# Chunked linear attention feeding a top-1 expert layer: loads of a chunk at other times and from two queues, a state update moved, a count folded into another product

## The chip, the core and the metric

The kernel runs on one core of one Trainium2 chip. The metric is device time in microseconds, from start to end of one execution; the figure used is the median of a few executions.

## What is computed

Two stages follow each other. The first is a linear attention with a decaying state, for 4 batches, 8 heads, 768 tokens and head size 48:

```python
for t in range(S):
    kt, vt, rt = (k[:, :, t], v[:, :, t], r[:, :, t])
    cur = np.einsum('bhd,bhe->bhde', u[None] * kt, vt)
    y[:, :, t] = np.einsum('bhd,bhde->bhe', rt, state + cur)
    state = w[None, :, :, None] * state + np.einsum('bhd,bhe->bhde', kt, vt)
```

Its output, 3072 tokens of 384 numbers, goes through a layer of 8 experts. Each token is sent to the expert with the largest logit, and there `out[mask] = gate_w[mask, None] * eom[mask, e, None] * (np.maximum(x[mask] @ w1[e], 0) @ w2[e])`, with the softmax weight of the chosen expert and a sigmoid gate.

## The kernel before, in words

The attention works on 24 chunks of 128 tokens, six along the sequence for each of four batches, with the batch running fastest. A chunk i is cut into two halves of 64 tokens, so that a decaying state is carried twice per chunk. The loop over chunks starts at line 1432, and its body is an order written out by hand: in the schedule in force each engine runs its instructions in just the order in which the code names them, and semaphores make it wait where data are not ready. Iteration i finishes the output of chunk i and prepares the chunks that follow. In it stand, in this order:

- `product(i+2)` on GpSimd (POOL, line 274), `scale(i+3)` on VectorE (DVE, line 261), `carry(i+1, 1)`, the second state update of chunk i+1 (a DVE addition that reads PSUM at line 336, then a POOL multiplication at line 337), and `keys(i+3)` on POOL (line 267).
- `strips(i+1)` (line 1378): small matmuls on TensorE (PE) for the bonus coefficients (line 373) and the router's logits (line 461), and two copies on ScalarE (ACT, lines 1388 and 469).
- `logits_t`, three transposes on PE (line 451) and an ACT copy (line 453), then `bonus(i+1)`, eight ACT instructions at line 382.
- `intra(i)` on PE (line 363) and `output(i)`: the DVE addition `x` at line 389, and the store of `x` to the scratch `x_d` from the SP queue (line 390).
- `state(i+2)` (PE, line 317) and `scores(i+1)` (PE, line 291), which fill one pair of PSUM banks; `carry(i+2, 0)` (lines 336 and 337); `inter(i+1)` (PE, line 353), which writes into the one pair of banks that the addition `x` of chunk i reads; and `causal(i+1)` (DVE, line 297), which masks the scores.

The pair of banks of `state` and `scores` has one buffer. So `state(i+2)` may start only when `causal(i)`, `carry(i+1, 0)` and `carry(i+1, 1)` have read the pair before. Likewise `inter(i+1)` may start only when `x` of chunk i has been read out.

Each chunk needs four loads, all issued from the SP queue by `load` (line 1272): the two halves of `rk` (192 KB each), `k` and `v` (200 KB each). They go into rings of 5, 4 and 5 buffers. In iteration i SP issues, behind the store of `x`: the second half of `rk` of chunk i+5, `v` of chunk i+5, `k` of chunk i+6 and, behind `causal`, the first half of `rk` of chunk i+6. No load is left from iteration 19 on.

The router's work is woven into the loop. Its tokens are taken in five groups of 5, 5, 4, 4 and 6 chunks (`GROUPS`). The program of a group (`Router.group`, line 477) is a generator that yields what its next step needs: a slot on DVE, a place for PE (`P`) or ACT (`A`), or a wait for PE's result (`W_`). `micro(i)` (line 1367) adds a credit from `BUDGETS` and runs DVE steps, 0.15 of credit each, until it is used up; `exchange` and `resume` run the others at fixed points of the iteration. A group's steps are: argmax and one-hot, the gate, the ranks' product on PE (lines 572 to 576), ranks and one-hot of positions with the weighting between them (`side`), the table's product on PE (line 631), and its additions to the table. For the group that ends at chunk 14 the generator `order` (line 713) runs before the gate: a PE product that sums the counts of each expert, a wait, and six DVE steps that find the fullest expert, whose number SP reads to load that expert's weights early (`load_raw`). From iteration 18 on, `weights0` splits these weights on ACT and POOL. After the loop come the experts, eight slots of matmuls.

Of the kernel before, what the change touches and what calls it, by code (L numbers as in the profile page):

```python
# [2 lines left out]

# [10 lines left out]
ALU = mybir.AluOpType  # L14
# [14 lines left out]
E, F = 8, 1024  # L29
# [20 lines left out]
ORDER_AT = 14  # L50
# [3 lines left out]
V, P, A, W_, SPLIT = "vector", "tensor", "scalar", "wait", "split"  # L54
SPLITS = {18: 1, 19: 1, 20: 1, 21: 1, 22: 2, 23: 2}
RINGS = {"rk": 5, "k": 4, "v": 5}
PARTS = {"rk": (0, RKW), "k": (RKW, RKW + NAT), "v": (RKW + NAT, IN)}
BUDGETS = [[0, 0.3], [12, 0.45], [18, 0.9], [20, 1.3]]
TAIL = 3
# [334 lines left out]
class Router:  # L394
# [82 lines left out]
    def group(self, ps, w, lg, i0, G, closing, last):  # L477
        nc, k = self.tc.nc, self.k
# [37 lines left out]
        cs = self.csum  # L516
        if not last:
# [5 lines left out]
            else:  # L523
                nc.vector.tensor_add(self.csum, self.csum, cs)
        if i0 + G == ORDER_AT and not self.plain:
            yield from self.order(ps, w)

# [47 lines left out]
        for c in range(G - 1):  # L575
            nc.tensor.matmul(cnt[:, (c + 1) * E :], k.ones16, oh16[:, c, :].unsqueeze(1).to_broadcast((C, G - 1 - c, E)), start=False, stop=(c == G - 2), skip_group_check=True)
        yield W_
        rk = mk("rk", E)
        cv = cnt.rearrange("p (c e) -> p c e", e=E)
# [132 lines left out]

    def order(self, ps, w):
        nc, k = self.tc.nc, self.k
        yield P
        pt = self.room[:, self.pt :]
        nc.tensor.matmul(pt[:, :E], k.ones, self.csum, start=True, stop=True)
        yield W_
        key = self.okey
        nc.vector.scalar_tensor_tensor(key, pt[:, :E], float(E), k.desc, op0=ALU.mult, op1=ALU.add)  # L720
        yield V
        top = w.tile([C, 1], F32, name="top")
        nc.vector.tensor_reduce(out=top, in_=key, axis=AX.X, op=ALU.max)
        yield V
        nc.vector.tensor_scalar(self.pm0, key, top, None, op0=ALU.is_ge)
        nc.vector.tensor_scalar(self.opm, key, top, None, op0=ALU.is_ge)
        yield V
        pe = w.tile([1, E], F32, name="pe0")
        nc.vector.tensor_mul(pe, self.opm[0:1], k.ip[0:1, :E])
        yield V  # L730
        pr = self.opr[0:1]
        nc.vector.tensor_reduce(out=pr, in_=pe, axis=AX.X, op=ALU.add)
        yield V
        nc.vector.tensor_copy(self.eid[:, 0:1], pr)
        self.after_order()
        yield V
# [513 lines left out]
def rwkv_top1_moe(ctx, tc, rkv, wu, wg, w1, w2, r, kk, v, w, u, out):  # L1250
    nc = tc.nc
# [10 lines left out]
    with ExitStack() as actx:  # L1262
# [8 lines left out]

        def load(nm, i, j=None):
            if i < NT:
                a, z = PARTS[nm]
                rows = slice(0, C) if j is None else slice(HB * j, HB * j + D)
                nc.sync.dma_start(rings[nm][i % RINGS[nm]][rows], rkv[i, rows, a:z])

# [81 lines left out]
        def mark():  # L1359
            gates[0] += 1  # L1360
            return gates[0]

        def resume():
            if pend and pend[0][1] == W_:
                pend[0][1] = V
# [8 lines left out]
        def exchange(kind):  # L1374
            if pend and pend[0][1] == kind and passed[0] > asked[0]:
                step()

        def strips(i, cs):
            lg = ps.tile([C, 512], F32, name="ps_cf", tag="lg", bufs=1)
            if i < NT:  # L1380
                att.coefs(i, lg)
            prog = None
            if i >= LATE:
                dst, prog = slot(i - LATE)
                pl = lg[:, 32 * E : SPARE]
                rt.logits_into(pl, xTs.pop(i - LATE))
            if i < NT:
                nc.scalar.copy(cs, lg[:, :E])  # L1388
            if i >= LATE:
                rt.logits_out(pl[:, : 2 * E], dst)  # L1390
            if prog:
                pend.append([prog, V])
            return lg
# [29 lines left out]
        att.state(1)  # L1423
        load("k", 1 + RINGS["k"])
        att.carry(1, 0)
        att.keys(2, nc.gpsimd)
        att.scale(2)
        x = None
        xTs = {}

        masked = mark()
        for i in range(NT):
            tail = i == NT - 1
            att.product(i + 2)
            att.scale(i + 3)
            att.carry(i + 1, 1)
            att.keys(i + 3, nc.gpsimd)
            micro(i)
            lg = strips(i + 1, cs[(i + 1) % 2])
            exchange(A)  # L1440
            if x is not None:
                xTs[i - 1] = rt.logits_t(ps, rw, x, "lg" if tail else "l", 1)
            exchange(P)
            att.bonus(i + 1, cs[(i + 1) % 2])
# [10 lines left out]
            exchange(P)  # L1455
            load("rk", i + RINGS["rk"], 1)
            load("v", i + RINGS["v"])
# [3 lines left out]
            att.state(i + 2)  # L1461
            load("k", i + 2 + RINGS["k"])
            att.scores(i + 1, range(NP - 1))
# [7 lines left out]
            passed[0] = summed  # L1471
            att.causal(i + 1)
            resume()
            load("rk", i + 1 + RINGS["rk"], 0)
            load_raw(1)
            micro(i, 2)
            if tail:
                ex.early_mm(ps, 0)
            for _ in range(SPLITS.get(i, 0)):
                weights0(pieces.pop(0))  # L1480
                micro(i)
            masked = mark()
        dst, prog = slot(NT - 2)
# [108 lines left out]
```

## Time and profile before

| | us |
|---|---|
| median of 3 runs | 401.1 (400.38 to 403.56) |
| profiled execution, its own time | 406.86 |
| its span, first to last instruction | 405.1 |

| engine | busy us | share of the span |
|---|---|---|
| PE | 358.9 | 89% |
| PE weight loads | 336.8 | 83% |
| DVE | 224.5 | 55% |
| ACT | 169.8 | 42% |
| POOL | 155.1 | 38% |

The table is an average over two stages with different limits: the chunks up to about 160 us, and the experts behind them. The profiled execution took 5.8 us longer than the median of the runs shown.

### The profile page before, as it was taken

Reading aid. Unit: us, or ns where it says so; the run is one execution under the profiler, and the core shown is the slowest. Engines: PE = TensorE matmul, PEld = TensorE weight load, DVE = VectorE, ACT = ScalarE, POOL = GpSimd, SP = SyncE. Lnnn points to the kernel's source line nnn. Section 1 sums busy time; section 2 is a strip of 40 time slices with the busy share of each in tenths; the row PEclk is TensorE's granted clock in tenths of the full one; section 3 lists DMA queues with packets and bytes.
Section 4 is the critical chain, followed back from the end, with each engine's and each line's share of the span. In section 5 each row is a group of like instructions: output and inputs, shape, how many; then the busy total and the mean of one; then the engine's idle time right before and its main releaser. Section 6 shows DMA issues by size and latency. Waiting matters only on the chain. (4 is left out here: it accounts for less than half of the span.)

```text
span 405.1 us, 12806 instructions
## 1 busy us (share of the span) xinstructions
PE 358.9 (89%) x5186; PEld 336.8 (83%) x5186; DVE 224.5 (55%) x565; ACT 169.8 (42%) x479; POOL 155.1 (38%) x214
## 2 busy tenths in 40 slices
PE   7796888786988867997999999999999999999990
PEld 3695777776877766887899999999999999999990
DVE  6553569668778762845763374374373653726600
ACT  3443444342444435522443263363553533634400
POOL 7754464643665617624150412312322412413010
PEclk9888998997998989999999999999999999999996
DMA  7946654763578206063372463454463563634110
GB/s 278 312 138 183 197 165 130 212 180 106 164 209 253 97 23 183 14 214 91 90 228 80 127 187 119 135 181 122 137 213 120 160 230 116 229 113 117 64 44 19
DMA packets 26516, 60.58 MB, mean 150 GB/s; under 512 B 4143, under 2 KB 13411, under 8 KB 26448
## 3 DMA queue, kind: packets, MB, share of 16 engines
q1 hardware_dynamic: 23024, 49.85, 40.6%
q0 software_dynamic: 3424, 9.82, 7.2%
q8 instruction: 43, 0.70, 0.7%
q14 instruction: 25, 0.20, 0.2%
HBM read 50.22 MB, written 9.76 MB: 148 GB/s over the span
## 5 line engine op out<-in xcount | busy, mean ns | idle before, releaser
L943 POOL DMA_INDIRECT out_dram<-yo,si x28 | 31.0, 1106 | 133.9 <-ACT yo L940 69.8
L906 PE MATMUL ps_h<-xh,w1h 128*128 128x384 f32 (+4 forms) x216 | 72.2, 334 | 0.8 <-DVE yo L942 0.8
L907 PE MATMUL ps_h<-xl,w1h 128*128 128x384 f32 (+4 forms) x216 | 70.7, 328 | 0.0
L908 PE MATMUL ps_h<-xh,w1l 128*128 128x384 f32 (+4 forms) x216 | 70.7, 327 | 0.0
L855 DVE TENSOR_TENSOR w1l<-raw,w1h 128x768 fp32r<-128x768 f32 x28 | 26.1, 955 | 61.0 <-ACT w1h L854 61.0
L915 ACT ACTIVATE hh<-ps_h 128x384 fp32r<-128x384 f32 (+4 forms) x72 | 34.1, 475 | 46.2 <-PE ps_h L908 45.4
L916 DVE SCALAR_TENSOR_TENSOR hl<-ps_h,hh 128x384 fp32r<-128x384 f32 (+4 forms) x72 | 38.4, 534 | 24.8 <-ACT hh L915 22.9
L382 ACT ACTIVATE vc<-v,cs 128x48 f32<-128x48 f32 x192 | 45.9, 324 | 0.1
L877 POOL DMA_INDIRECT xg<-x_d,gi x28 | 30.8, 1099 | 38.4 <-PE ps_xt L889 26.0
L337 POOL TENSOR_TENSOR T<-Ts,sq 128x192 f32<-128x192 f32 x40 | 20.2, 506 | 64.7 <-DVE Ts L336 59.7
L968 PE MATMUL ps_o<-w2h,hh 128*128 128x384 f32 x128 | 43.8, 342 | 0.7 <-ACT yo L940 0.7
L970 PE MATMUL ps_o<-w2h,hl 128*128 128x384 f32 x128 | 42.8, 335 | 0.0
L969 PE MATMUL ps_o<-w2l,hh 128*128 128x384 f32 x128 | 42.8, 334 | 0.0
L906 PEld LDWEIGHTS ps_h<-xh,w1h 128*128 128x128 f32 x216 | 40.7, 189 | 1.5 <-issue 1.1
L907 PEld LDWEIGHTS ps_h<-xl,w1h 128*128 128x128 f32 x216 | 40.8, 189 | 0.1
L908 PEld LDWEIGHTS ps_h<-xh,w1l 128*128 128x128 f32 x216 | 40.7, 188 | 0.1
L1388 ACT COPY cs<-ps_cf 128x8 f32<-128x8 f32 x24 | 4.0, 165 | 75.4 <-PE ps_cf L461 67.2
L363 PEld LDWEIGHTS ps_y<-v,A 64*64 64x64 f32 x768 | 27.3, 147 | 7.1 <-issue 3.0
L363 PE MATMUL ps_y<-v,A 64*64 64x64 f32 x768 | 31.1, 234 | 2.3 <-DVE A L297 1.4
L274 POOL TENSOR_TENSOR rk<-rk 128x512 f32<-128x512 f32 x24 | 30.5, 1272 | 0.7 <-DMA rk<-in_rkv_dram 0.7
L261 DVE TENSOR_TENSOR rk<-rk,ps_tb 128x1024 f32<-128x1024 f32 x24 | 28.9, 1211 | 0.7 <-ACT ps_tb L228 0.7
L291 PE MATMUL ps_a<-rk 48*64 48x64 f32 x768 | 25.8, 239 | 3.3 <-issue 2.9
(206 smaller groups left out, 722.8 us busy)
## 6 DMA issues: line engine op xcount, KB each, us to landing
raw<-in_w_dram SPq DMA_DIRECT2D x64, 384.0 KB, 3.5
rk<-in_rkv_dram SPq DMA_DIRECT2D x38, 192.0 KB, 4.0
k<-in_rkv_dram SPq DMA_DIRECT2D x24, 200.0 KB, 4.5
v<-in_rkv_dram SPq DMA_DIRECT2D x24, 200.0 KB, 3.6
x_d<-x SPq DMA_DIRECT2D x24, 192.0 KB, 1.9
rk<-in_rkv_dram SPq DMA_DIRECT2D x5, 512.0 KB, 5.6
xg<-x_d,gi POOLq DMA_INDIRECT x28
out_dram<-yo,si POOLq DMA_INDIRECT x28
```

The source lines that it names most:

```text
L363: nc.tensor.matmul(o, A[rows, j, q, :], self.values(i, rows, 2 * q + j), start=(i < B and c == 0 and q == 0), stop=(q == NP - 1), skip_gro ...
L382: nc.scalar.activation(vc[:, h, :], vt[:, h, :], AF.Copy, scale=cs[:, h : h + 1])
L877: nc.gpsimd.indirect_dma_start(out=self.xg[q][:n], out_offset=None, in_=self.x_d[:n_x, :], in_offset=bass.IndirectOffsetOnAxis(ap=self.rt. ...
L906: nc.tensor.matmul(o, wh[:, j, fs], xh, start=(j == 0), stop=False)
L907: nc.tensor.matmul(o, wh[:, j, fs], xl, start=False, stop=False)
L908: nc.tensor.matmul(o, wl[:, j, fs], xh, start=False, stop=(j == KC - 1))
L915: nc.scalar.activation(hh, o, AF.Relu)
L916: nc.vector.scalar_tensor_tensor(hl, o, 0.0, hh, op0=ALU.max, op1=ALU.subtract)
L943: nc.gpsimd.indirect_dma_start(out=self.out, out_offset=bass.IndirectOffsetOnAxis(ap=self.rt.si[:n, q, s : s + 1] if s else self.rt.si0[:n ...
L968: nc.tensor.matmul(o, hh, wh, start=(f == 0), stop=False)
L969: nc.tensor.matmul(o, hh, wl, start=False, stop=False)
L970: nc.tensor.matmul(o, hl, wh, start=False, stop=(f == FC - 1))
```

## The change

The loads of `rk`'s second half and of `k` move from the SP queue to the ACT queue. The first stands in `strips`, between its two ACT copies; the second behind `logits_t`, in front of `bonus`. `k` of chunk i+5 is now asked for in iteration i (it was chunk i+6, later in the iteration), and one load of `k` leaves the part ahead of the loop. The other two loads and the store stay on SP. `carry(i+2, 1)` goes right behind `causal(i+1)`, at the end of the iteration before the one in which it stood. In `order` the PE product and its wait are gone: the sum of the counts is one more matmul among those of the ranks' product, and the six DVE steps of `order` take the places between the steps of the ranks that the weighting had; the weighting follows them. The credits of `BUDGETS` fall from 0.45 to 0.4 for chunks 12 to 17, from 0.9 to 0.4 for chunk 18, and from 1.3 to 0.9 from chunk 20 on; chunk 19 keeps 0.9.

```diff
--- before.py
+++ after.py
@@ -1,5 +1,6 @@
 from collections import deque
 from contextlib import ExitStack
+from itertools import chain
 
 import concourse.bass as bass
 import concourse.tile as tile
@@ -55,7 +56,7 @@
 SPLITS = {18: 1, 19: 1, 20: 1, 21: 1, 22: 2, 23: 2}
 RINGS = {"rk": 5, "k": 4, "v": 5}
 PARTS = {"rk": (0, RKW), "k": (RKW, RKW + NAT), "v": (RKW + NAT, IN)}
-BUDGETS = [[0, 0.3], [12, 0.45], [18, 0.9], [20, 1.3]]
+BUDGETS = [[0, 0.3], [12, 0.4], [19, 0.9]]
 TAIL = 3
 REST = 2
 ROT = (("lg", 1), ("y", 2), ("g", 1), ("y", 2))
@@ -522,8 +523,7 @@
                 nc.vector.tensor_copy(self.csum, cs)
             else:
                 nc.vector.tensor_add(self.csum, self.csum, cs)
-        if i0 + G == ORDER_AT and not self.plain:
-            yield from self.order(ps, w)
+        ordering = i0 + G == ORDER_AT and not self.plain
 
         def expert():
             nc.vector.tensor_scalar(self.eidx[:, cols], m, -1.0, float(E), op0=ALU.mult, op1=ALU.add)
@@ -574,7 +574,11 @@
             nc.tensor.matmul(cnt, k.ones16, rep(self.csum16), start=False, stop=(G == 1), skip_group_check=True)
         for c in range(G - 1):
             nc.tensor.matmul(cnt[:, (c + 1) * E :], k.ones16, oh16[:, c, :].unsqueeze(1).to_broadcast((C, G - 1 - c, E)), start=False, stop=(c == G - 2), skip_group_check=True)
+        if ordering:
+            nc.tensor.matmul(pc[:, G * E : (G + 1) * E], k.ones, self.csum, start=True, stop=True, skip_group_check=True)
         yield W_
+        if ordering:
+            side = chain(self.order(w, pc[:, G * E : (G + 1) * E]), side)
         rk = mk("rk", E)
         cv = cnt.rearrange("p (c e) -> p c e", e=E)
         if based:
@@ -710,14 +714,10 @@
             yield V
             nc.vector.tensor_copy(self.sc0, self.t0[:, 1, :EARLY])
 
-    def order(self, ps, w):
+    def order(self, w, tot):
         nc, k = self.tc.nc, self.k
-        yield P
-        pt = self.room[:, self.pt :]
-        nc.tensor.matmul(pt[:, :E], k.ones, self.csum, start=True, stop=True)
-        yield W_
         key = self.okey
-        nc.vector.scalar_tensor_tensor(key, pt[:, :E], float(E), k.desc, op0=ALU.mult, op1=ALU.add)
+        nc.vector.scalar_tensor_tensor(key, tot, float(E), k.desc, op0=ALU.mult, op1=ALU.add)
         yield V
         top = w.tile([C, 1], F32, name="top")
         nc.vector.tensor_reduce(out=top, in_=key, axis=AX.X, op=ALU.max)
@@ -1269,11 +1269,11 @@
         pin = fctx.enter_context(tc.tile_pool(name="att_in", bufs=1))
         rings = {nm: [pin.tile([C, z - a], F32, name=f"{nm}_{n}") for n in range(RINGS[nm])] for nm, (a, z) in PARTS.items()}
 
-        def load(nm, i, j=None):
+        def load(nm, i, j=None, eng=nc.sync):
             if i < NT:
                 a, z = PARTS[nm]
                 rows = slice(0, C) if j is None else slice(HB * j, HB * j + D)
-                nc.sync.dma_start(rings[nm][i % RINGS[nm]][rows], rkv[i, rows, a:z])
+                eng.dma_start(rings[nm][i % RINGS[nm]][rows], rkv[i, rows, a:z])
 
         for nm, i in (("rk", 0), ("k", 0), ("rk", 1), ("v", 0), ("k", 1), ("rk", 2), ("v", 1), ("k", 2)):
             load(nm, i)
@@ -1375,7 +1375,7 @@
             if pend and pend[0][1] == kind and passed[0] > asked[0]:
                 step()
 
-        def strips(i, cs):
+        def strips(i, cs, between=lambda: None):
             lg = ps.tile([C, 512], F32, name="ps_cf", tag="lg", bufs=1)
             if i < NT:
                 att.coefs(i, lg)
@@ -1386,6 +1386,7 @@
                 rt.logits_into(pl, xTs.pop(i - LATE))
             if i < NT:
                 nc.scalar.copy(cs, lg[:, :E])
+            between()
             if i >= LATE:
                 rt.logits_out(pl[:, : 2 * E], dst)
             if prog:
@@ -1421,10 +1422,10 @@
         att.product(1)
         att.pa = att.banks("ps_a", "at")
         att.state(1)
-        load("k", 1 + RINGS["k"])
         att.carry(1, 0)
         att.keys(2, nc.gpsimd)
         att.scale(2)
+        att.carry(1, 1)
         x = None
         xTs = {}
 
@@ -1433,13 +1434,13 @@
             tail = i == NT - 1
             att.product(i + 2)
             att.scale(i + 3)
-            att.carry(i + 1, 1)
             att.keys(i + 3, nc.gpsimd)
             micro(i)
-            lg = strips(i + 1, cs[(i + 1) % 2])
+            lg = strips(i + 1, cs[(i + 1) % 2], lambda: load("rk", i + RINGS["rk"], 1, nc.scalar))
             exchange(A)
             if x is not None:
                 xTs[i - 1] = rt.logits_t(ps, rw, x, "lg" if tail else "l", 1)
+            load("k", i + 1 + RINGS["k"], None, nc.scalar)
             exchange(P)
             att.bonus(i + 1, cs[(i + 1) % 2])
             micro(i)
@@ -1453,13 +1454,11 @@
             resume()
             exchange(A)
             exchange(P)
-            load("rk", i + RINGS["rk"], 1)
             load("v", i + RINGS["v"])
             load_raw(1)
             if i + 1 < NT:
                 att.pa = att.banks("ps_a", "at")
             att.state(i + 2)
-            load("k", i + 2 + RINGS["k"])
             att.scores(i + 1, range(NP - 1))
             att.carry(i + 2, 0)
             micro(i, 2)
@@ -1470,16 +1469,17 @@
             att.scores(i + 1, range(NP - 1, NP))
             passed[0] = summed
             att.causal(i + 1)
+            att.carry(i + 2, 1)
             resume()
             load("rk", i + 1 + RINGS["rk"], 0)
             load_raw(1)
             micro(i, 2)
+            masked = mark()
             if tail:
                 ex.early_mm(ps, 0)
             for _ in range(SPLITS.get(i, 0)):
                 weights0(pieces.pop(0))
                 micro(i)
-            masked = mark()
         dst, prog = slot(NT - 2)
         rt.logits_out(rt.logits_mm(ps, xTs.pop(NT - 2), "lg"), dst)
         assert not pend, (i, pend)
```

## Rows read from the trace of the kernel before

**Rows 1.** Windows of the span: busy us of each engine, TensorE clock, DMA share, GB/s

```profile
27.20:31.70 4.50, 4.50 (x165) 4.06 (x163) 3.00 (x5) 2.70 (x13) 3.38 (x5) 1.00 0.55 161
31.70:41.00 9.30, 5.90 (x177) 5.27 (x172) 3.00 (x5) 3.09 (x15) 4.42 (x6) 0.82 0.58 168
...
200.00:360.00 160.00, 159.20 (x911) 155.99 (x910) 81.78 (x121) 72.40 (x128) 43.25 (x39) 1.00 0.50 160
```

**Rows 2.** Timeline of DVE, the addition `x` at L389 (24 of them): start us, us

```profile
22.96 0.56 DVE L389 TENSOR_TENSOR x<-ps_y,vc 128x384 f32<-128x384 f32 x1 [1.78 <-PE ps_y L363]
27.49 0.56 DVE L389 TENSOR_TENSOR x<-ps_y,vc 128x384 f32<-128x384 f32 x1 [0.44 <-issue]
31.83 0.56 DVE L389 TENSOR_TENSOR x<-ps_y,vc 128x384 f32<-128x384 f32 x1 [0.45 <-issue]
...
158.22 0.56 DVE L389 TENSOR_TENSOR x<-ps_y,vc 128x384 f32<-128x384 f32 x1 [0.22 <-PE ps_y L363]
```

**Rows 3.** Waits of PE: us in total, times, longest us

```profile
PE ps_cf L373 <- issue: 7.2, 3, 3.4
PE ps_a L317 <- issue: 6.4, 5, 3.2
...
PE ps_a L291 <- issue: 2.9, 4, 1.4
...
PE ps_y L353 <- issue: 1.5, 2, 0.9
```

**Rows 4.** Timeline of PE around 35 us; idle before in brackets

```profile
33.31 0.50 PE L373 MATMUL ps_cf<-uw,rk 128*64 128x64 f32 x9
37.21 0.58 PE L373 MATMUL ps_cf<-uw,rk 128*64 128x64 f32 x6 [3.40 <-issue]
```

**Rows 5.** DMA queues in the 0.1 us from 34.9 us on

```profile
q8 instruction: 1, 0.02, 63.1%
```

**Rows 6.** The page, part 1 (engines) and part 3 (queues: packets, MB)

```profile
PE 358.9 (89%) x5186; PEld 336.8 (83%) x5186; DVE 224.5 (55%) x565; ACT 169.8 (42%) x479; POOL 155.1 (38%) x214
...
q8 instruction: 43, 0.70, 0.7%
```

**Rows 7.** Timeline of DVE, 89 to 97 us (17 router steps from 90.37 on)

```profile
89.77 0.69 DVE L297 TENSOR_TENSOR A<-ps_a,diag 128x512 f32<-128x512 f32 x1 [0.49 <-PE ps_a L291]
90.37 0.19 DVE L585 TENSOR_TENSOR rk<-ps_room,oh 128x40 f32<-128x40 f32 x1
...
93.73 0.17 DVE L552 CAST parts<-ps_room 128x5 bf16<-128x5 f32 x1
93.81 1.22 DVE L261 TENSOR_TENSOR rk<-rk,ps_tb 128x1024 f32<-128x1024 f32 x1
94.95 0.35 DVE L336 TENSOR_TENSOR Ts<-ps_a,T 128x192 f32<-128x192 f32 x1
...
96.14 0.56 DVE L389 TENSOR_TENSOR x<-ps_y,vc 128x384 f32<-128x384 f32 x1
```

**Rows 8.** Timeline of PE at three places in the loop

```profile
95.40 1.12 PE L317 MATMUL ps_a<-v,k 64*64 64x64 f32 x30 [3.21 <-issue]
...
96.95 0.31 PE L353 MATMUL ps_y<-T,rk 48*64 48x64 f32 x1
...
145.62 0.44 PE L631 MATMUL ps_room<-rhs,ohp 128*128 128x160 bf16 x4 [3.54 <-DVE rhs L626]
```

**Rows 9.** Timeline of SP, first and last of the four loads of an iteration

```profile
103.71 0.38 SPq L1276 DMA_DIRECT2D rk<-in_rkv_dram  x1
...
105.12 0.38 SPq L1276 DMA_DIRECT2D rk<-in_rkv_dram  x1
```

**Rows 10.** Timeline of ACT, the first copy of the same iteration

```profile
105.85 0.17 ACT L1388 COPY cs<-ps_cf 128x8 f32<-128x8 f32 x1 [2.45 <-PE ps_cf L461]
```

**Rows 11.** Waits of ACT: us in total, times, longest us

```profile
ACT cs L1388 <- PE ps_cf L461: 67.2, 21, 6.7
```

**Rows 12.** DMA issues: KB each, median us to landing

```profile
k<-in_rkv_dram SPq DMA_DIRECT2D x24, 200.0 KB, 4.5
```

## The prediction

> **What bounds the kernel now.** I read the windows first, then the DVE additions that mark the chunks, then PE's waits, and last the timelines around the longest of these. From 200 to 360 us PE is busy 159.20 of 160 us [rows 1]: the experts are PE's own work, the change touches none of it, and whatever the chunks save comes through to the end. The chunks are different. The addition `x` of chunk 1 starts at 22.96 us and that of chunk 23 at 158.22 us [rows 2], so 22 intervals take 135.26 us, 6.15 us each. One undisturbed interval (27.49 to 31.83) takes 4.34 us, with PE busy all through the window around it [rows 1, 2]. Some 1.8 us a chunk, 40 us in all, are therefore waits and slow stretches. They are of three kinds.
>
> First, PE stops in the middle of a line with nothing of its data missing ("issue" in the waits): 7.2 + 6.4 + 2.9 + 1.5 = 18.0 us at four lines, 14 times [rows 3]. The longest lies between two matmuls of one line: nine run at 33.31 us, the next at 37.21 us, 3.40 us idle [rows 4]. What comes in between is one packet of the queue named instruction, at 34.9 us [rows 5]. That queue moved 43 packets, 0.70 MB, so 16 KB each; PE and its weight loads are 2 x 5186 instructions, 241 for a packet [rows 6]. I read this as PE's own code arriving late: a block lasts about 241 instructions, three quarters of a chunk's work, and when its packet is held up behind data PE stands still. Where that wait is long the clock falls too: in 31.70 to 41.00 us its mean is 0.82 [rows 1].
>
> Second, two of the five waits at line 317 are DVE's. At 95.40 us `state` starts after 3.21 us, just as the second state update (94.95 us, 0.35 us) ends [rows 7, 8]. Ahead of that update DVE had, behind the mask, 17 router instructions from 90.37 us to 93.81 us, 0.20 us each, and `scale` (1.22 us) [rows 7]. The other such wait is 1.80 us, in chunk 8. Without these two, 18.0 - 5.0 = 13.0 us in 12 waits are left to the first kind.
>
> Third, the router's PE products wait for DVE: 3.54 us at 145.62 us, at the table's product of the fourth group [rows 8].
>
> **The second state update behind the mask.** It adds and removes no instruction. `state` no longer waits for micro steps and `scale`, which could give back at most 3.21 + 1.80 = 5.0 us. But the next gate is close: `inter` needs `x`, and DVE reaches `x` only after the same 17 steps, `scale` and two more steps. In chunk 13 `x` runs at 96.14 us for 0.56 us, so to 96.70; `inter` starts at 96.95 us [rows 7, 8]. With `state` and 24 of the scores' matmuls done early, it starts 0.25 us earlier, and the next state update and mask follow perhaps 0.5 us earlier. Twice that is about 1 us; I take 1 us, with 0 to 5.0 us as ends. POOL is moved past as well: the multiplication of this update now stands in front of `product(i+2)`, and so waits for the mask. `product` then starts up to 1.5 us later, but its reader, the coefficients' matmuls, stands most of an iteration behind it; I cost that at nothing. Should this cover go, DVE's 0.69 us mask and 0.35 us update [rows 7] would be added in each of 22 chunks, 23 us at the very worst.
>
> **The loads at other times.** No byte is saved. Before, the four loads leave SP between 103.71 and 105.12 us, in 1.4 us [rows 9]. Afterwards `v` leaves at the first of these times, half of `rk` about where the last did, the other half behind ACT's copy at 105.85 us [rows 10], and `k` about 1 us later, behind `xT`: 3.2 us for the same 784 KB. The pile that an instruction packet meets is lower, so its wait should shrink; by how much no row shows. The ends are the whole 13.0 us, and a loss of the same size if a second queue beside the first holds the packets up more. Waits are not proportional to bursts, and with shorter chunks the DMA engines (0.55 to 0.58 busy in such windows [rows 1]) have less rest, so I take a third, 4 us, and 1 us for the clock that then falls less often (the window at 0.82 lost some 9.3 x 0.18 = 1.7 us, and PE's longest wait is the one most likely to shrink).
>
> ACT gains 19 + 19 = 38 issues (chunks 5 to 23, two each). At the 0.38 us of SP's [rows 9] that is 14.4 us, 0.76 us in an iteration. It hides beside ACT's waits for the coefficients, 67.2 us in 21 times [rows 11]. Queued behind an issue are the logits' copy and the eight `vc`; `vc(i+1)` is wanted only by the `x` of the next iteration. So I cost it at nothing, at 14.4 us if the cover were gone. SP loses the same issues, and waits in its old place no more for `state(i+2)` before it can ask for the last half of `rk`.
>
> The Trainium skill's page "Runtime: NRT & Kernel Launch" (Instruction fetch mechanics) says that code comes in 16 KB blocks fetched ahead, and that the cost of crossing a block is mostly hidden. This trace agrees on the 16 KB [rows 6] and not on the hiding [rows 4]. Its page "DMA: Bandwidth & Descriptors" (Issuing engines are not separate DMA queues) says that DMAs issued from several engines run on the same DMA engines and only save the sequencer's issue time. By these two, this part gives 0 and not 5 us; that case is the first rival below.
>
> **The count folded in, and the credits.** One PE product with its wait goes, one small matmul is added behind the ranks' product. Counting the credits by the code, the third group's ranks come in iteration 16 instead of 17. There 13 instructions (ranks and `order` in turn) now stand between the first state update and the mask, 13 x 0.20 = 2.6 us, and some 1.7 us behind it; before, the 17 instructions of one burst stood behind the mask of iteration 17. From `x` of chunk 16 to that of 17, DVE then has about 0.56 + 0.35 + 2.6 + 0.69 + 0.35 + 1.7 + 1.22 + 1.1 = 8.6 us, what the burst cost before one chunk later: 0 in sum. In the fourth group the ranks' burst moves in iteration 20 from behind the mask to ahead of it, 19 instructions, some 4.2 us. PE has about 2 us of work there (`inter`, coefficients, logits, transposes), so it then waits 2 to 2.5 us for the mask. In return the table's inputs are ready before `x` of chunk 21, and the 3.54 us wait [rows 8] goes, with the slow stretch behind it. I take 2 us, between -3 (the new wait comes, the old one stays) and 5.
>
> **The sum.** 1 + 5 + 0 + 2 = 8 us off the profiled execution, which has a span of 405.1 us and took 406.9 us: 399 us. The median of the runs shown is 401.1, 5.8 lower, so part of the waits that I count was longer in the profiled execution; I take 7 us off the median: 394 us. The ends from the terms, -3 and +5 for the credits, 0 and 5 for the update, -13 and +14 for the loads, can't all fall together.
>
> **The rivals.** *The loads are hidden anyway.* Instruction packets come as late as before, because the DMA engines move the same 784 KB in each chunk, or because the PE time saved only lengthens the wait at the next gate, `x`. For it: in chunk 13 PE is gated by DVE and not by code. Against it: 3.40 us of pure idle with a packet in the middle. Only the update and the credits are left, with part of them lost at that gate: 2 us less than before, 399 us.
>
> *The second queue makes code later.* With SP's and ACT's loads both waiting at the DMA engines, each instruction packet waits longer. A full chunk's 161 matmuls are 322 instructions with their weight loads, 1.3 packets of 241 [rows 6], so some 25 over the 19 iterations with loads; 0.5 us more on each is 12.5 us, less 3 for the other parts: 410 us. It decides from about 0.12 us a packet on. For it: `k` and half of `rk` now leave while PE is in its densest part, and the packet of 34.9 us shows how far one can be held back. Against it: the bursts get shorter.
>
> *`k` comes too late.* It is asked for in iteration i and used by `keys` at the head of iteration i+2, after some 1.6 chunks, 6.9 us at the fastest, and lands 4.5 us after its issue [rows 12]. If ACT stands in its 6.7 us wait [rows 11] or the landing takes longer, POOL's queue stops, and `state` behind it. One microsecond in half of 19 chunks makes it 394 + 10 = 404 us. This is also the way in which the change doesn't do what it says: loads spread in the code that ACT in fact issues late and close to SP's next ones.
>
> **How the numbers follow.** The forecast has 0.58, the hidden loads 0.26, the second queue 0.12, the late `k` 0.04. The measurement can tell about 1% from no change, so from 397.1 to 405.1 us counts as the same. The forecast lies under that; the hidden loads and the late `k` lie in it; the second queue lies above. A few of the forecast's cases end within 1% and a few of the hidden ones under it, which cancel, and the late `k` can also be worse than 1 us, so I halve it: faster 0.58, same 0.28, slower 0.14. The range goes from 385, where two thirds of the 13.0 us and the upper ends of the other terms come in, to 404, where the hidden and the late cases end and most of the second queue's is left out.
>
> **What would show it.** In the profile of the changed kernel: waits of PE named issue at lines 373, 317, 291 and 353 of together under 12 us (18.0 before), none above 2.5 us; no wait at line 317 right behind line 336; the mean interval of `x` under 5.9 us; the wait at line 631 in the loop gone and one for the mask at line 363 of 2 to 3 us in its place; ACT's wait for the coefficients some 14 us shorter, with no wait for `vc` at `x`. It would be wrong if the issue waits stay at 18 us with the loads spread, if `keys` on POOL waits for a DMA, or if `x` is still as late in chunks 8, 13 and 17 and everything ahead of it only waits there.

## The result and the profile after

| | before | after |
|---|---|---|
| median of 14 runs each, us | 402.96 (400.38 to 407.7) | 398.84 (393.76 to 400.92) |
| ratio | | 0.9869 [0.9833, 0.9905] |
| profiled execution (span), us | 406.86 (405.1) | 396.13 (394.4) |

The change takes 1.31% off, 0.95 to 1.67%. Of some 403 us that is 5.3 us; the forecast was 7 us. The ratio leaves out runs more than 1.5% above the fastest of their kernel; over all 14 the medians differ by 4.1 us, 1.0%. The spans of the two profiled executions differ by 10.7 us, so waits and stretches read from this pair make the change look larger than it is.

The page of the changed kernel, parts 1, 3 and 6, to be held against [rows 6, 12]:

```profile
PE 355.6 (90%) x5186; PEld 334.5 (85%) x5186; DVE 223.8 (57%) x565; ACT 172.5 (44%) x479; POOL 152.7 (39%) x214
...
q10 hardware_dynamic: 3952, 7.63, 8.3%
...
q8 instruction: 43, 0.70, 0.8%
...
v<-in_rkv_dram SPq DMA_DIRECT2D x24, 200.0 KB, 4.5
x_d<-x SPq DMA_DIRECT2D x24, 192.0 KB, 3.1
k<-in_rkv_dram ACTq DMA_DIRECT2D x19, 200.0 KB, 4.2
```

PE has the same 5186 matmuls and as many code packets. 7.63 MB now go through a queue of ACT's, q10, and `k` lands 4.2 us after its issue there, 4.5 before.

Waits of PE in the changed kernel, the answer to [rows 3] (line numbers are one higher; 374 is coefs, 318 state, 292 scores, 354 inter, 364 intra):

```profile
PE ps_y L354 <- DVE x L390: 9.7, 5, 3.7
PE ps_cf L374 <- issue: 5.0, 2, 3.2
PE ps_y L364 <- DVE A L298: 3.6, 2, 2.8
PE ps_y L364 <- issue: 1.7, 2, 1.2
...
PE ps_a L318 <- issue: 0.8, 2, 0.5
PE ps_a L292 <- issue: 0.6, 1, 0.6
```

The issue waits at coefs, state, scores and inter fall from 18.0 to 5.0 + 0.8 + 0.6 = 6.4 us; with intra, where they were 0.8 us, from 18.8 to 8.1 us. But a new name stands at the top: `inter` waits 9.7 us for `x`, five times, where before that wait came to 1.8 us in all, as the same view of the kernel before has it:

```profile
PE ps_y L353 <- DVE x L389: 1.8, 2, 1.1
```

Two of the five, with the wait for the mask and the code stop that remained, on PE's timeline:

```profile
30.95 0.50 PE L374 MATMUL ps_cf<-uw,rk 128*64 128x64 f32 x9
34.61 0.39 PE L374 MATMUL ps_cf<-uw,rk 128*64 128x64 f32 x6 [3.15 <-issue]
...
62.03 0.78 PE L354 MATMUL ps_y<-T,rk 48*64 48x64 f32 x32 [2.38 <-DVE x L390]
...
92.58 0.69 PE L354 MATMUL ps_y<-T,rk 48*64 48x64 f32 x32 [3.71 <-DVE x L390]
...
136.44 1.15 PE L364 MATMUL ps_y<-v,A 64*64 64x64 f32 x32 [2.79 <-DVE A L298]
137.56 0.69 PE L635 MATMUL ps_room<-rhs,ohp 128*128 128x160 bf16 x4
```

The 3.15 us stop is the one of [rows 4] again: nine matmuls of the same line, then six. The last two rows answer to [rows 8]: the table's product of the fourth group runs without a wait, and 2.79 us for the mask stand ahead of it.

DVE around chunk 13 in the changed kernel, the answer to [rows 7]:

```profile
85.53 0.69 DVE L298 TENSOR_TENSOR A<-ps_a,diag 128x512 f32<-128x512 f32 x1 [0.49 <-PE ps_a L292]
86.14 0.35 DVE L337 TENSOR_TENSOR Ts<-ps_a,T 128x192 f32<-128x192 f32 x1
86.40 0.19 DVE L589 TENSOR_TENSOR rk<-ps_room,oh 128x40 f32<-128x40 f32 x1
...
89.47 1.22 DVE L262 TENSOR_TENSOR rk<-rk,ps_tb 128x1024 f32<-128x1024 f32 x1
...
91.97 0.56 DVE L390 TENSOR_TENSOR x<-ps_y,vc 128x384 f32<-128x384 f32 x1
```

The update now starts 0.61 us behind the start of the mask, where it was 5.18 us. From mask to `x` DVE still needs 6.44 us (6.37 before), and so PE stands 3.71 us at `inter` where it stood 3.21 us at `state`.

Two windows of the changed kernel, the start of the loop and the experts (the second answers to [rows 1]):

```profile
16.00:24.00 8.00, 7.94 (x253) 7.12 (x254) 5.85 (x10) 4.59 (x20) 5.50 (x7) 1.00 0.96 243
...
200.00:350.00 150.00, 150.00 (x866) 147.65 (x865) 74.86 (x111) 67.83 (x121) 36.17 (x34) 1.00 0.48 155
```

The experts are PE's own work as before; the first window comes up again in the last section. On DVE's timeline of the changed kernel, `x` of chunks 0, 1 and 23, and below them `x` of chunk 0 in the kernel before:

```profile
15.86 0.55 DVE L390 TENSOR_TENSOR x<-ps_y,vc 128x384 f32<-128x384 f32 x1
19.85 0.56 DVE L390 TENSOR_TENSOR x<-ps_y,vc 128x384 f32<-128x384 f32 x1
...
150.15 0.56 DVE L390 TENSOR_TENSOR x<-ps_y,vc 128x384 f32<-128x384 f32 x1
```

```profile
15.27 0.55 DVE L389 TENSOR_TENSOR x<-ps_y,vc 128x384 f32<-128x384 f32 x1
```

The 22 intervals take 130.30 us, 5.92 each (6.15 before). Chunk 23 comes 158.22 - 150.15 = 8.07 us earlier; the other 2.6 us between the spans lie behind it, in the experts, and in the twelve other profiles this last part takes 243.9 to 249.1 us, so they are not put down to the change. Stage by stage, from `x` to `x`, in us: 0 to 1: 7.7 to 4.0; 1 to 4: 18.2 to 18.5; 4 to 12: 45.6 to 45.5; 12 to 15: 21.6 to 19.1; 15 to 19: 22.9 to 23.5; 19 to 23: 26.9 to 23.7.

### The profile page after: what moved, and what is told of

Read it like the earlier page. It is cut to its first block, busy times and chain, and to the rows that moved or that the text cites. A ratio compares the mean times of both kernels' runs of the same rounds, so it can differ in the third digit from the quotient of the medians.

```text
span 394.4 us, 12818 instructions
## 1 busy us (share of the span) xinstructions
PE 355.6 (90%) x5186; PEld 334.5 (85%) x5186; DVE 223.8 (57%) x565; ACT 172.5 (44%) x479; POOL 152.7 (39%) x214
## 3 DMA queue, kind: packets, MB, share of 16 engines
q10 hardware_dynamic: 3952, 7.63, 8.3%
## 5 line engine op out<-in xcount | busy, mean ns | idle before, releaser
L943 POOL DMA_INDIRECT out_dram<-yo,si x28 | 29.5, 1053 | 133.6 <-ACT yo L940 70.6
L877 POOL DMA_INDIRECT xg<-x_d,gi x28 | 29.9, 1069 | 38.4 <-PE ps_xt L889 25.9
L364 PE MATMUL ps_y<-v,A 64*64 64x64 f32 x768 | 31.9, 239 | 5.3 <-DVE A L298 3.6
L364 PEld LDWEIGHTS ps_y<-v,A 64*64 64x64 f32 x768 | 28.1, 151 | 9.8 <-DVE A L298 4.6
L855 DVE TENSOR_TENSOR w2l<-raw,w2h 128x768 fp32r<-128x768 f32 x28 | 26.8, 957 | 3.2 <-ACT w2h L854 2.0
```

What stands on the lines that cost most here:

```text
L364: nc.tensor.matmul(o, A[rows, j, q, :], self.values(i, rows, 2 * q + j), start=(i < B and c == 0 and q == 0), stop=(q == NP - 1), skip_gro ...
L855: (eng or nc.vector).tensor_sub(lo, self.raw[i][:, cs], hi)
```

## The experiments

My theory was that of the prediction: the loads at other times give most, because code arrives sooner; the rival that they are hidden anyway, and only the router's steps and the update count. All ratios are to the kernel before, run beside it on the same chip; the runs were on three chips, on which the kernel before has medians of 407.9, 403.0 and 402.9 us. "Code waits" are PE's issue waits up to 160 us at the five lines named above, in the one profile of each kernel (two of the changed one). In a kernel with the update in its old place they hold some that are DVE's, so they are compared only with that said.

**The three parts alone.** The loads alone:

```diff
-                nc.sync.dma_start(rings[nm][i % RINGS[nm]][rows], rkv[i, rows, a:z])
+                eng.dma_start(rings[nm][i % RINGS[nm]][rows], rkv[i, rows, a:z])
...
-        load("k", 1 + RINGS["k"])
...
+            lg = strips(i + 1, cs[(i + 1) % 2], lambda: load("rk", i + RINGS["rk"], 1, nc.scalar))
...
+            load("k", i + 1 + RINGS["k"], None, nc.scalar)
...
-            load("rk", i + RINGS["rk"], 1)
...
-            load("k", i + 2 + RINGS["k"])
```

> Only the loads are changed (times and second queue). Theory of the prediction: this is the largest part, 4 to 5 us off, 398 us beside 403 for the kernel before; waits of PE named issue at the lines of state, scores, inter, intra and coefficients fall from 18.0 to about 10 us, though the two long waits of state on the second update stay. Rival (loads hidden anyway): within 1 us of the kernel before and issue waits of 16 us or more. On the start: if the interval from the first to the second x (7.69 us before, 3.99 after the whole change) is short because one load of k less stands ahead of the loop, it is about 4 us here too; if the second update is what shortens it, it stays near 7.7.

Measured: 0.996 [0.9909, 1.001]. The code waits are 17.0 us (18.8 before), in a profile of a run of 409.18 us where the median is 407.31; 5.4 and 5.0 us of them, those right behind the second update, are DVE's. Both figures are nearer to the rival's than to the theory's. The first interval of `x` is 5.14 us, at neither of the two marks.

The update alone:

```diff
+        att.carry(1, 1)
...
-            att.carry(i + 1, 1)
...
             att.causal(i + 1)
+            att.carry(i + 2, 1)
```

> Only the second state update is moved behind the mask. Theory of the prediction: 1 us off, at most 2, as x is the next gate: the waits of state behind the update go (5.0 us at that line) and come back as waits of inter for x, some 8 us in all. Rival: the update is what pays, since it also shortens the start, where the first interval of x falls from 7.69 to 4 us with the clock at 1.00; then 4 us off.

Measured: 0.9994 [0.9949, 1.0038]. Its waits of PE show what became of it; the code waits are 13.5 us, all of them code's now (13.8 before, once DVE's 5.0 are out):

```profile
PE ps_y L353 <- DVE x L389: 9.9, 5, 3.0
PE ps_cf L373 <- issue: 4.8, 3, 1.8
PE ps_y L353 <- issue: 2.8, 2, 1.5
PE ps_a L317 <- issue: 2.7, 5, 0.9
```

The 5.0 us at `state` are gone, and 9.9 - 1.8 = 8.1 us have come up at `inter`.

The steps alone (the count folded in, the credits, and the mark for the mask, which in the changed kernel stands ahead of the last lines of the loop):

```diff
-BUDGETS = [[0, 0.3], [12, 0.45], [18, 0.9], [20, 1.3]]
+BUDGETS = [[0, 0.3], [12, 0.4], [19, 0.9]]
...
+        if ordering:
+            nc.tensor.matmul(pc[:, G * E : (G + 1) * E], k.ones, self.csum, start=True, stop=True, skip_group_check=True)
         yield W_
+        if ordering:
+            side = chain(self.order(w, pc[:, G * E : (G + 1) * E]), side)
```

> Only the count folded into the ranks' product and the lower credits. Theory of the prediction: 2 us off; the 3.54 us wait at the table's product of the fourth group is gone, a wait of 2 to 3 us for the mask stands in the iteration before it. Rival: the burst ahead of the mask costs as much as the one behind it did, and the time is within 1 us of the kernel before.

Measured: 0.9953 [0.9907, 0.9999], the only one of the three alone whose interval lies under 1, if barely. The exchange of waits came as forecast: PE doesn't wait for the table's inputs, and 2.8 us for the mask.

**One queue.** The whole change, with the two moved loads issued by SP at the same places of the code:

```diff
-            lg = strips(i + 1, cs[(i + 1) % 2], lambda: load("rk", i + RINGS["rk"], 1, nc.scalar))
+            lg = strips(i + 1, cs[(i + 1) % 2], lambda: load("rk", i + RINGS["rk"], 1, nc.sync))
...
-            load("k", i + 1 + RINGS["k"], None, nc.scalar)
+            load("k", i + 1 + RINGS["k"], None, nc.sync)
```

> The whole change, but all loads are issued from SP at the same places in the order. If the times of the loads matter and not the queue: within 1 us of the whole change (399 us), issue waits of PE about 8 us as there. If the second queue pays (SP stands behind x and behind the waits of its own stores when a load's place comes): 2 us or more above the whole change and issue waits back above 12 us. If the second queue costs (more packets ahead of code): 1 to 3 us below the whole change.

Measured: 0.9877 [0.9809, 0.9945], and 0.9869 with two queues. Neither the second queue nor ACT's 38 issues cost or give anything that these runs can tell; the intervals leave room for some 3 us either way. The code waits are 12.6 us, above the 12 us that were to mark a second queue that pays, so this one profile points another way than the time.

**The whole, and the whole without one part.** The changed kernel once more, to set the next three against it:

> The whole change once more, on the chip of the next three, to set them against it: 1.3% below the kernel before, as in its first runs. If PE's issue waits differ from execution to execution, this profile shows another sum than the first one's 8.1 us: up to 13 us would say that the fall from 18.8 was partly chance.

Measured: 0.9869 [0.9814, 0.9925], code waits 9.3 us.

Without the loads (the first diff of this section undone):

```diff
-            lg = strips(i + 1, cs[(i + 1) % 2], lambda: load("rk", i + RINGS["rk"], 1, nc.scalar))
+            lg = strips(i + 1, cs[(i + 1) % 2])
...
+            load("rk", i + RINGS["rk"], 1)
...
+            load("k", i + 2 + RINGS["k"])
```

> The whole change with the loads left where they were. If the parts add up (loads alone gave 0.4%): 0.8 to 0.9% below the kernel before, 1.5 to 2 us above the whole change. If the loads pay more once the other waits are gone (5 us, as predicted): 0.2% below the kernel before, and issue waits of PE 13 us or more. If the loads are hidden: as fast as the whole change.

Measured: 0.9923 [0.9876, 0.997]. Its issue waits of PE:

```profile
PE ps_cf L374 <- issue: 3.4, 2, 2.1
PE ps_a L318 <- issue: 1.9, 4, 0.6
PE ps_y L364 <- issue: 1.6, 3, 0.9
PE ps_y L354 <- issue: 1.5, 1, 1.5
...
PE ps_a L292 <- issue: 0.8, 2, 0.6
```

Together 9.2 us, against 8.1 and 9.3 us in the two profiles of the whole. So the code waits fell as far with the loads left where they were: the fall that I had forecast is there, but spreading the loads is not needed for it.

Without the update:

```diff
+            att.carry(i + 1, 1)
...
-            att.carry(i + 2, 1)
```

> The whole change with the second state update left where it was. If the parts add up (the update alone gave 0.06%): within 1 us of the whole change, although the first interval of x is back at 5 us or more. If the update pays only beside the others, since it takes PE's wait at state away and the loads take the wait for code away: 2 us or more above the whole change.

Measured: 0.9948 [0.9894, 1.0003], some 3 us above the whole, the sign named for an update that pays only beside the others. The first interval of `x` is 5.58 us.

Without the steps:

```diff
-BUDGETS = [[0, 0.3], [12, 0.4], [19, 0.9]]
+BUDGETS = [[0, 0.3], [12, 0.45], [18, 0.9], [20, 1.3]]
...
+            yield from self.order(ps, w)
...
-            side = chain(self.order(w, pc[:, G * E : (G + 1) * E]), side)
```

> The whole change without the folded count and with the old credits. If the parts add up (the steps alone gave 0.47%): 2 us above the whole change, 0.8% below the kernel before, and the wait of PE's table product of the fourth group is back (2 to 3.5 us). If the loads and the update do the work: as fast as the whole change.

Measured: 0.996 [0.991, 1.0009], with the wait for the table's product back:

```profile
PE ps_room L631 <- DVE rhs L626: 3.5, 1, 3.5
```

Alone, the three parts give 0.40, 0.06 and 0.47%, together 0.93%. Taken out of the whole, they cost 0.54, 0.79 and 0.91%, together 2.24%, with the whole at 1.31% between. Each of the first three has half a per cent of uncertainty, each of the differences somewhat more. That the update is worth more beside the other two than alone is suggested by this, not settled.

**The credits apart from the fold.** The whole with the old credits:

```diff
-BUDGETS = [[0, 0.3], [12, 0.4], [19, 0.9]]
+BUDGETS = [[0, 0.3], [12, 0.45], [18, 0.9], [20, 1.3]]
```

> The whole change with the old credits, so that of the steps only the folded count is left. If the fold pays and the credits are only what makes room for it: within 1 us of the whole change (1.3% below the kernel before). If the credits pay: 1.5 to 3 us above the whole change; the wait of PE for the mask in iteration 20 is then over 4 us instead of 2.8, since more of the ranks' burst stands ahead of the mask.

Measured: 0.9954 [0.9914, 0.9994]. Against the whole's 0.9869 from other runs, the credits carry some 0.85%, with over half a per cent of uncertainty. With the fold kept this kernel is hardly better than the one without any of the steps (0.996): by itself the fold moves the time by nothing that the runs can tell. The exchange of waits is the fold's already: no wait at the table's product, and 3.65 us for the mask in iteration 20 (over 4 us was expected), which the lower credits bring down to 2.79 us. From chunk 19 to 23, where the credits differ most, this kernel takes 25.8 us; the whole takes 23.7 and 24.2 us.

**The start alone.** The stretch from `x` of chunk 0 to that of chunk 1 had shrunk the most. To see what that is worth, only the first of the second updates goes ahead of the loop:

```diff
+        att.carry(1, 1)
...
-            att.carry(i + 1, 1)
+            if i:
+                att.carry(i + 1, 1)
```

> The kernel before, with one instruction pair moved: the second state update of chunk 1 stands ahead of the loop instead of behind the first scale in it. If the shorter start (first interval of x 7.7 us before, 4 us with the update or the whole change, clock 0.57 against 1.00 in 16 to 24 us) is most of what the update and the loads give: first interval about 4 us, 2.5 to 3.5 us below the kernel before (0.6 to 0.9%). If what is won at the start is given back later at the next gates, as the update alone suggests: within 1 us.

Measured: 1.0025 [0.9987, 1.0063]. `x` of chunks 1, 4 and 23 on DVE's timeline of this kernel:

```profile
20.81 0.56 DVE L389 TENSOR_TENSOR x<-ps_y,vc 128x384 f32<-128x384 f32 x1
...
37.11 0.56 DVE L389 TENSOR_TENSOR x<-ps_y,vc 128x384 f32<-128x384 f32 x1 [1.96 <-ACT xT L453]
...
158.22 0.56 DVE L389 TENSOR_TENSOR x<-ps_y,vc 128x384 f32<-128x384 f32 x1
```

The same chunk 4 on DVE's timeline of the kernel before:

```profile
41.13 0.56 DVE L389 TENSOR_TENSOR x<-ps_y,vc 128x384 f32<-128x384 f32 x1 [5.57 <-issue]
```

The first interval is 5.82 us, 1.9 us shorter than before (4 us was expected). Chunk 4 is 4.02 us ahead of the kernel before, chunk 23 comes at the very same 158.22 us [rows 2]. In this profile what the start gains is given back in the chunks behind it, and the time shows no gain; so the 3.7 us that the stage list above shows from chunk 0 to 1 are not simply part of the 5.3 us.

**The amount of load traffic.** More: the whole with a further 200 KB load in each of the 19 iterations, into buffers that nobody reads.

```diff
+        spare = [pin.tile([C, NAT], F32, name=f"spare_{n}") for n in range(2)]
...
             load("v", i + RINGS["v"])
+            if i + RINGS["v"] < NT:
+                nc.sync.dma_start(spare[i % 2], rkv[i + RINGS["v"], :, RKW + NAT : IN])
```

> The whole change with one more load of 200 KB in each chunk (v a second time, into spare buffers that nobody reads), issued from SP behind v. If PE's wait for code hangs on the traffic of the loads, as the prediction took it: issue waits of PE rise from 8 to 9.5 us to 15 us or more, and the time by 4 to 8 us. If it does not: issue waits below 12 us, time within 2 us of the whole change.

Measured: 0.9992 [0.995, 1.0034], the whole gain used up, some 5 us. Its waits of PE:

```profile
PE ps_y L354 <- DVE x L390: 5.3, 5, 1.7
PE ps_y L364 <- issue: 4.0, 5, 1.0
PE ps_y L354 <- issue: 3.8, 4, 1.3
...
PE ps_a L292 <- issue: 3.5, 3, 2.6
PE ps_cf L374 <- issue: 3.0, 2, 1.8
PE ps_a L318 <- issue: 2.4, 3, 1.7
```

Less: the whole without the loads of `v` from chunk 5 on, so that later chunks work on the `v` of earlier ones.

```diff
-            load("v", i + RINGS["v"])
```

> The whole change without the loads of v from chunk 5 on (the values of older chunks are used in their place, so the outputs of later chunks differ and the experts may be filled otherwise; the chunks' part of the trace is what counts). If PE's wait for code hangs on the traffic of the loads: issue waits fall to 5 us or less and the chunks from the fourth to the fifteenth get 2 us shorter. If it does not: 8 us or more, and the same intervals of x.

Measured: 0.9804 [0.9732, 0.9876], from only four runs, of a kernel that computes other numbers. From `x` of chunk 4 to that of chunk 15 it takes 62.6 us, 2 us less than the whole (64.6 and 64.4), as expected if the traffic counts. Its waits of PE:

```profile
PE ps_y L354 <- DVE x L390: 9.9, 6, 3.2
...
PE ps_cf L374 <- issue: 1.6, 1, 1.6
...
PE ps_a L318 <- issue: 1.4, 4, 0.6
...
PE ps_a L292 <- issue: 1.0, 1, 1.0
PE ps_y L364 <- issue: 0.7, 1, 0.7
```

With 584, 784 and 984 KB a chunk the code waits are 4.7, 8.1 to 9.3, and 16.7 us, and the ratios 0.9804, 0.9869 and 0.9992. So the amount of load traffic does hold the code up; the time shows it for the added loads, while for the omitted ones the intervals overlap. The wait for `x` is 9.9, 9.7 and 5.3 us: where code comes latest, `x` is more often ready by the time PE gets there.

**The code waits by part.** Without what stands right behind the second update and is DVE's, they are 11.6 to 15.4 us in the five kernels without the steps (before 13.8, loads alone 11.6, update alone 13.5, start alone 15.4, whole without the steps 12.1). With the steps, at the same 784 KB, they are 7.8 to 9.7 us (steps alone 7.8, whole 8.1 and 9.3, without the loads 9.2, without the update 9.7, with the old credits 9.1); one queue, 12.6 us, falls out of line. So in these single profiles most of the fall goes with the steps and little with the loads. One stop can be named: behind `x` of chunk 17 PE stands 1.25 to 1.80 us at coefs in all five profiles without the fold, and in none of the nine with it.

## Why the prediction was right, and where its sum was off

**The direction and the range** held: 398.84 us lies between 385 and 404, and 0.9869 is faster by over 1%. Of the 4.8 us between 394 and 398.84, 402.96 - 401.1 = 1.9 us are the three runs that the forecast started from, which lay under the median of fourteen. The other 2.9 us are the sum (1.7 us by the ratio's 5.3). That the total came so near is partly luck: its largest term was some 3 us too high, and the other two gave more in company than they were put at.

**The loads, forecast at 4 + 1 us, are the term that was mis-sized.** They measured 0.40% alone and 0.54% in company, 1.6 to 2.2 us of some 403; alone, the interval ends at 0.91% = 3.7 us. The mechanism is there: more bytes in flight make code later. The step that failed is "the pile that an instruction packet meets is lower, so its wait should shrink", taken at a third of 13.0 us: with the loads alone code's part of the waits is 11.6 us, 13.8 before by the same count, and the large fall comes with the steps. The bytes are the same 784 KB, and they flow in shorter chunks, which the prediction named as a reason for caution and weighed too low; that this is the reason is argued, not shown. The 1 us for the clock shows nowhere: from 10 to 150 us the mean granted clock is 0.90 in both profiles, before and after, 0.96 in the second profile of the whole and 0.86 with the loads alone.

What a long stop consists of can be read further than the prediction took it. This is the queues' view of the changed kernel from 32.1 to 32.2 us:

```profile
q8 instruction: 1, 0.02, 67.5%
```

A window counts the packets that start in it, with their whole time, as a share of 16 engines' time in the window. This one takes 0.675 x 16 x 0.1 = 1.08 us, so it ends at some 33.2 us. PE stopped at 30.95 + 0.50 = 31.45 us, 0.7 us before the packet started, and went on at 34.61 us, 1.4 us after its end. In the kernel before it is the same: the packet that starts at 34.9 us takes 1.01 us, and PE is on at 37.21 us [rows 4, 5], some 1.25 us after its end. The 43 packets take 1.1 us on average, so these two were not slow on the way; they started late. When each had been asked for, no row shows. The prediction took PE's stops for late code from one packet, and the two profiles bear it out: 16 stops of 0.5 us or more with no other cause end 1.2 to 1.7 us after the end of a packet of this queue, while the 3.21 us of `state` that were put down to DVE end 4.0 us after one. The Trainium skill's page "Runtime: NRT & Kernel Launch" (Instruction fetch mechanics) calls the crossing of a block mostly hidden; the 3.15 us in the changed kernel again say that it is not always so here.

The rival of the hidden loads was thus nearer on this part than the forecast. Its total, 2 us or 0.5%, lies outside the measured 0.95 to 1.67%, because the other parts gave more than it allowed. The sign that I named for the forecast, code waits under 12 us, came true (6.4 us at the four lines), yet it was a poor sign: the kernel without the moved loads shows it too, 7.6 us. "None above 2.5" failed in this profile (3.15 us) and held in the second one of the same kernel (1.8 us); so did the mean interval of `x` under 5.9 us (5.92, then 5.87).

**The update, 1 us,** was right in its reason: `state`'s wait turns into `inter`'s wait for `x`. Alone it gave 0.06%, 0.2 us; in company 0.79%. A sign named for being wrong, `x` as late as before in chunks 8 and 13, came true in part: up to `x` of chunk 8 it takes 7.93 us from that of chunk 7 before, 8.07 and 8.34 us in the two profiles of the whole; up to chunk 13 it takes 9.36 us before, 8.13 and 8.92 after. The cover named for the moved multiplication held: from 16 to 160 us PE waits nowhere for POOL.

**The count and the credits, 2 us,** measured 0.47% alone (1.9 us) and 0.91% in company. The exchange came nearly as forecast: the 3.54 us wait at the table's product for 2 to 2.5 us at the mask, measured 2.79 us. For the third group, which the fold moves a chunk ahead, the sum was 0, with 8.6 us from `x` of chunk 16 to that of 17; it took 7.68 us. From `x` of chunk 16 to that of 18 the nine profiles with the fold take 12.5 to 14.1 us and the five without it 14.4 to 15.2, among them the stop at coefs named above. So the 0 should have been a gain of some 1 us, less than the run with the old credits can tell from nothing.

**ACT's issues, 0 us,** were hidden as said. This is ACT's wait for the coefficients in the changed kernel, to be held against [rows 11]:

```profile
ACT cs L1388 <- PE ps_cf L462: 53.9, 21, 6.5
```

It is 13.3 us shorter; 14.4 us was the forecast for the issues. DVE's waits at `x` name no `vc`; those that name ACT's `xT` grow from 1.0 to 4.4 us, and two, 2.7 us together, now name a load of `rk`. The second queue's rival (410 us) fell with the run on one queue, 0.9877 beside 0.9869, as the page "DMA: Bandwidth & Descriptors" of the Trainium skill (Issuing engines are not separate DMA queues) would have it. The late `k` fell too: among POOL's waits from 16 to 160 us none names a load of `k`, and one, of 1.4 us, a load of `rk`.

**What stays open:** how the 1.31% divides among the parts, and how much of it is the credits'. Also why the start's gain is given back, and why the code waits fall with the steps beyond the one stop; a PE that stands at `x` gives code time to arrive, but the update alone, with 9.9 us at `x`, left them at 13.5 us, so this is not enough of a reason. Most kernels have one profile, and with one queue the code waits differ by 3 to 4.5 us from the whole's though the time does not.

## What to carry to other kernels

A wait named issue can shrink while the time hardly moves: ask which gate is next, and count only what passes it. When code arrives late behind data, look at the bytes first: 200 KB more in each chunk cost 1.2% here, and moving the same bytes about gave some half a per cent, not clear of the noise. Before crediting a part with the shorter stretch that stands beside it in a profile, make the run with that part alone.

## What the runs showed of the hardware

A packet of code, 16 KB, took 1.1 us on average, and from its end to PE's next matmul it took another 1.2 to 1.7 us in the 16 stops of the two profiles. The transfers left on SP land later in the changed kernel than before: `v` after 4.5 us (3.6 before), the store of `x` after 3.1 us (1.9 before). The second queue is not needed for that: with one queue and the loads at the same places it is 4.2 and 3.8 us. Whether it costs time was not tried by itself.

From 16 to 24 us the granted clock was 0.57 in the kernel before, mostly the lower of its two levels (1.2 and 2.4 GHz), with PE busy 7.44 of 8 us:

```profile
16.00:24.00 8.00, 7.44 (x183) 6.74 (x175) 3.00 (x5) 2.45 (x10) 4.81 (x5) 0.57 0.53 145
```

In the 8 us ahead of that it was 1.00, with PE busy 5.26 us. In the changed kernel it was 1.00 from 16 to 24 us and 0.79 in the 8 us ahead, with PE busy 6.41 us. The kernel with the start alone had 1.00 in both and was no faster for it.

An issue of a DMA on ACT, from its timeline in the changed kernel:

```profile
36.51 0.92 ACTq L1276 DMA_DIRECT2D k<-in_rkv_dram  x1
```

The one of the iteration before takes 0.34 us, as half of the 19 issues of `k` there do, near SP's 0.38 us [rows 9]; this one takes 0.92 us.
